# Adjacent weight rows per partition in a decode step with attention and a gated FFN

## The chip, the cores and the metric

The kernel runs on one core of a Trainium2 chip. In the profiles PE is TensorE (PEld its weight loads), DVE VectorE, ACT ScalarE, POOL GpSimd and SP SyncE. The metric is the device time of one launch in microseconds. Most executions of a kernel agree closely; some fall into a slower state, a few us longer at the same work, and are marked as slow (here: over 1.5% above the fastest run of the same kernel). Medians below are of all runs unless fast runs are named. Ratios and their intervals are from fast runs of the same rounds, so they aren't quite the ratio of the medians quoted beside them.

## The reference, cut to what matters

A layer with two parallel branches is run forward and backward: decode attention (4 sequences, one token, 32 query heads, 8 K/V heads, window of 1,024) and a gelu-gated FFN. Outputs are the result and the gradients of x, both caches, wq, wo, w_gate, w_up, w_down.

```python
xn = _layernorm(x)
q = xn @ wq                                   # wq: 512 x 4096
o = softmax(q k^T * 128**-0.5) v              # the last 1024 of 4096 positions
out = x + o @ wo + (gelu(xn @ w_gate) * (xn @ w_up)) @ w_down   # wo: 4096 x 512
# and the vjp of it for grad_out; F = 1792, D = 512, all bf16
```

The cache gradients are zero outside the window: 50 MB of the 81 MB that the kernel writes are zeros.

## The kernel before: the parts that matter

`evac` moves a finished product from PSUM, where TensorE leaves it, to SBUF, the working memory, on ScalarE (ACT) or VectorE (DVE), whichever is less loaded by its own estimate. That estimate counts elements.

```python
def evac(out, in_, n, half=False, eng=None):
    eng = "dve" if half else eng
    ca, cd = (190 + n) / 1.2, (120 + (n / 2 if half else n)) / 0.96
    ...
        last.append(nc.scalar.copy(out=out, in_=in_))
    ...
    return nc.vector.tensor_copy(out=out, in_=in_)

# the small inputs, then the FFN weights; rows 128 apart go to one partition
for eng, dst, src in ((nc.sync, dy_b, grad_out), (nc.scalar, x_b, A_x)):
    eng.dma_start(out=dst[:], in_=bass.AP(tensor=src.tensor, offset=src.offset,
                                          ap=[[D, B], [0, RB], [1, D]]))
nc.sync.dma_start(out=wd_sb[:], in_=B_w_down.rearrange("(c p) n -> p c n", p=P))
nc.sync.dma_start(out=wg_sb[:], in_=B_w_gate.rearrange("(c p) f -> p c f", p=P))
...
# pre(t): do, per head, from the transposed wo
for i in range(2):
    for c in range(ND):
        nc.tensor.matmul(dq_ps[:, 0, 2 * h2 + i, :], lhsT=woT[:, i, c, :], rhs=dyT[:, c, :], ...)
...
# dw_gate, dw_up: one piece of the output rows of chunk c
nc.tensor.matmul(mps[:, 0:n, :]..., lhsT=xnm[:, i, c * P:(c + 1) * P], rhs=s_r[:, 0:n, :]..., ...)
evac(held["osb"][:, 0:n, i, :], mps[:, 0:n, :], n * P)      # runs of 128 elements
```

Zeros are issued on ACT's queue at fixed places of the program, the first at the end of the FFN; loads go out on SP's queue, the other stores on GpSimd's.

## Time and profile before

| | before |
|---|---|
| median of 3 runs | 291.73 us (291.46 to 292.57) |
| profiled execution | span 287.5 us, mean granted clock 0.849 |
| bytes | 112.38 MB at a mean of 391 GB/s |
| end of the FFN (first zeros issued) | 41.16 us |
| last store of dw_up issued | 78.69 us |

The page gives busy shares of each engine, then the span in 40 slices: each digit is a busy share in tenths, and DMA is the mean of the core's 16 DMA engines. Read the DMA row first; the prediction shows it. One line of the costliest groups names the source line, engine, operation, output and input, count, then busy time, mean ns of one, idle time before and its cause.

```profile
L92 ACT CAST osb_g<-dwg_ps 128x384 bf16<-128x384 f32 (+1 forms) x30 | 14.5, 534 | 17.6 <-PE dwg_ps L621 8.1
```

Thirty pieces of dw_gate and dw_up keep ACT busy for 14.5 us; one takes 0.53 us in the mean of both sizes (neighbours overlap a little, so the mean times thirty is more than the busy time).

### The profile page before, as it was taken

The page shows a single profiled execution, that of the slowest core. Times are in us where ns is not written, and L with a number is a line of the kernel's source. Part 1 is how long each engine was busy: PE and PEld are TensorE (multiplying, and loading weights), DVE is VectorE, ACT ScalarE, POOL GpSimd, SP SyncE. Part 2 cuts the span into 40 slices and gives each one's busy share as a digit, 9 for nine tenths or more (in the row PEclk, how much of TensorE's full clock was granted, in tenths as well). Part 3 has the DMA queues.
Part 4 walks back from the last instruction along what each step waited for, and adds up shares of the span by engine and source line. Part 5 has one row for each costly group of instructions (what it writes and reads, how often), then busy time and mean ns, then how long its engine had stood idle before and what let it go on. Part 6 is the DMA issues. An engine that isn't in the chain of part 4 may idle for free.

```text
span 287.5 us, 6821 instructions
## 1 busy us (share of the span) xinstructions
PE 206.9 (72%) x2956; PEld 141.5 (49%) x2956; DVE 144.9 (50%) x310; ACT 113.7 (40%) x217; POOL 66.7 (23%) x84
## 2 busy tenths in 40 slices
PE   1397994983977999545689996546998679597710
PEld 0386882652644765333357654323665355364310
DVE  5484572333564567312626674126476525537770
ACT  1201653443442467312424563134355444336610
POOL 7000130441303152311033323110252132112410
PEclk9996899597897899795958898959799969959975
DMA  5999999999999999999998999999999999999897
GB/s 138 381 389 376 385 399 421 413 403 429 423 426 427 413 372 401 435 415 427 416 419 330 327 363 429 426 427 411 415 413 380 395 390 412 406 415 360 337 393 295
DMA packets 30182, 112.38 MB, mean 391 GB/s; under 512 B 1537, under 2 KB 7689, under 8 KB 26057
## 3 DMA queue, kind: packets, MB, share of 16 engines
q10 hardware_dynamic: 4612, 50.46, 41.9%
q1 hardware_dynamic: 17732, 30.81, 29.4%
q0 software_dynamic: 7808, 30.67, 27.3%
q8 instruction: 23, 0.38, 0.5%
q14 instruction: 7, 0.05, 0.0%
HBM read 30.93 MB, written 81.01 MB: 389 GB/s over the span
## 4 chain that ended last, share of the span: by engine, by line
PE 47%; DMA 28%; DVE 14%; issue 4%; ACT 2%; POOL 1%; SPq 0%; DVEq 0%; ACTq 0%; POOLq 0%
DMA out_dram<-osb_o 14%; PE T_ps L336 9%; PE kv_ps L444 7%; DMA out_dram<-stg_dv 4%; DVE T_sb L94 4%; PE S_ps L341 4%; DMA wd_sb<-in_B_w_down_dram 4%; DMA out_dram<-osb_d 3%; PE od_ps L416 3%; PE woT_ps L288 3%; PE wqT_ps L508 3%; DMA out_dram<-osb_g 2%; PE acc_ps L181 2%; PE wgT_ps L648 2%; PE wdT_ps L536 2%
## 5 line engine op out<-in xcount | busy, mean ns | idle before, releaser
L94 DVE COPY T_sb<-T_ps 128x1024 bf16<-128x1024 bf16 x64 | 44.2, 691 | 34.2 <-PE T_ps L336 33.7
L92 ACT CAST stg_dv<-kv_ps 128x512 bf16<-128x512 f32 x52 | 28.8, 589 | 43.2 <-PE kv_ps L444 42.8
L92 ACT CAST stg_dk<-kv_ps 128x512 bf16<-128x512 f32 x46 | 25.0, 588 | 15.4 <-PE kv_ps L444 13.1
L336 PE MATMUL T_ps<-ident,vb 128*128 128x128 bf16 x256 | 26.1, 251 | 6.6 <-DVE osb_q L94 6.6
L336 PEld LDWEIGHTS <-vb 128*128 128x128 bf16 x256 | 20.0, 114 | 12.7 <-issue 8.9
L92 ACT CAST osb_q<-dwq_ps 128x512 bf16<-128x512 f32 x25 | 13.6, 589 | 30.4 <-DMA out_dram<-osb_o 20.1
L336 PE MATMUL T_ps<-ident,kb 128*128 128x128 bf16 x256 | 24.4, 228 | 0.5 <-ACT stg_dk L92 0.3
L336 PEld LDWEIGHTS <-kb 128*128 128x128 bf16 x256 | 18.1, 101 | 12.4 <-issue 5.0
L444 PE MATMUL kv_ps<-domr,P_q 128*128 128x512 bf16 x64 | 23.9, 435 | 0.0
L444 PE MATMUL kv_ps<-qmr,dS_q 128*128 128x512 bf16 x64 | 20.9, 410 | 1.5 <-ACT stg_dk L92 1.0
L92 ACT CAST osb_g<-dwg_ps 128x384 bf16<-128x384 f32 (+1 forms) x30 | 14.5, 534 | 17.6 <-PE dwg_ps L621 8.1
L94 DVE COPY woT<-woT_ps 128x1024 bf16<-128x1024 bf16 x16 | 11.1, 692 | 17.2 <-PE woT_ps L288 17.2
L478 PE MATMUL dwq_ps<-od_r,xnm 128*128 128x256 bf16 x64 | 12.5, 320 | 6.8 <-DVE osb_q L94 6.6
L352 POOL TENSOR_TENSOR dS_q<-dS_b,qmsk 128x1024 bf16<-128x1024 bf16 x4 | 7.5, 1884 | 34.3 <-DVE dS_b L405 34.3
L92 ACT CAST osb_o<-dwo_ps 128x512 bf16<-128x512 f32 x23 | 12.7, 588 | 7.0 <-PE dwo_ps L463 6.8
L341 PE MATMUL S_ps<-T_sb,dom 128*32 128x256 bf16 x128 | 10.5, 310 | 5.1 <-DVE T_sb L94 5.1
L98 POOL DMA_DIRECT2D out_dram<-osb_q x8 | 5.8, 731 | 34.6 <-ACT osb_q L92 34.6
L94 DVE COPY wqT<-wqT_ps 128x1024 bf16<-128x1024 bf16 x16 | 11.0, 687 | 5.5 <-PE wqT_ps L508 5.3
L508 PEld LDWEIGHTS <-wq_sb 128*128 128x128 bf16 x128 | 11.1, 120 | 5.3 <-issue 4.3
L94 DVE CAST osb_q<-dwq_ps 128x512 bf16<-128x512 f32 x7 | 4.7, 689 | 16.9 <-DMA out_dram<-osb_o 16.9
L98 POOL DMA_DIRECT2D out_dram<-stg_dv x8 | 6.2, 774 | 30.4 <-ACT stg_dv L92 30.4
L94 DVE CAST stg_dk<-kv_ps 128x512 bf16<-128x512 f32 x18 | 12.0, 685 | 2.4 <-PE kv_ps L444 1.2
(187 smaller groups left out, 381.1 us busy)
## 6 DMA issues: line engine op xcount, KB each, us to landing
out_dram<-ztile ACTq DMA_DIRECT2D x8, 3072.0 KB, 16.5
out_dram<-ztile ACTq DMA_DIRECT2D x16, 1536.0 KB, 15.3
kb<-in_A_k_cache_dram SPq DMA_DIRECT2D x8, 1024.0 KB, 17.1
vb<-in_A_v_cache_dram SPq DMA_DIRECT2D x8, 1024.0 KB, 49.5
out_dram<-stg_dv POOLq DMA_DIRECT2D x8, 1024.0 KB, 10.1
out_dram<-stg_dk POOLq DMA_DIRECT2D x8, 1024.0 KB, 8.4
wo_sb<-in_A_wo_dram SPq DMA_DIRECT2D x4, 1024.0 KB, 10.2
wq_sb<-in_A_wq_dram SPq DMA_DIRECT2D x4, 1024.0 KB, 14.2
```

Of the source, the lines that this page charges most:

```text
L92: last.append(nc.scalar.copy(out=out, in_=in_))
L94: return nc.vector.tensor_copy(out=out, in_=in_)
L98: d = eng.dma_start(out=out, in_=in_)
L181: nc.tensor.matmul(ps[:, c, :], lhsT=lf(c), rhs=rhs, start=(k == 0), stop=(k == len(terms) - 1))
L288: nc.tensor.transpose(wT_ps[:, i, c, :], wo_sb[:, 2 * h2 + i, c * P:(c + 1) * P], ident[:])
L336: nc.tensor.transpose(T_ps[:, j, :], blks[(t, g)][:, b, j, :], ident[:])
L341: nc.tensor.matmul(ps[q * RG:(q + 1) * RG, :], lhsT=lf[:, s * RG:(s + 1) * RG], rhs=T_sb[:, q * WQ:(q + 1) * WQ], start=(g == 0 and b == 0 ...
L352: nc.gpsimd.tensor_tensor(out=dst[:], in0=src[:].unsqueeze(1).broadcast_to([P, NQ, WQ]), in1=qmsk[:].unsqueeze(2).broadcast_to([P, NQ, WQ] ...
L416: nc.tensor.matmul(od_ps[b * RB:b * RB + rep, k, g, :], lhsT=pT[:, jj, c0:c0 + rep], rhs=blks[(t, g)][:, b, j, :], start=(j == 0), stop=(j ...
L444: nc.tensor.matmul(mps[:].rearrange("p b d -> p (b d)"), lhsT=src[:, q, jj * P:(jj + 1) * P], rhs=mr[:, g].rearrange("p b d -> p (b d)"), ...
L478: nc.tensor.matmul(mps[:, i].rearrange("p g d -> p (g d)"), lhsT=xnm[:, i2 * 2 + i, c * P:(c + 1) * P], rhs=dq_r[:].rearrange("p g d -> p ...
L508: nc.tensor.transpose(wT_ps[:, i, c, :], wq_sb[:, c, h * Dh:(h + 1) * Dh], ident[:])
```

## The change

The intent is larger transfers. If a partition holds adjacent rows of a weight, they are one contiguous run in memory. So wo gets 8 adjacent rows per partition, w_down 14, w_gate, w_up and wq 4. The price is that the index of a row is now partition times k plus k', and everything that meets this index has to follow it: the columns of w_gate and w_up are taken 14 apart, the outputs dw_gate and dw_up are assembled 14 apart, do is computed as 4 rows, written 8 apart and transposed back, and o is spread over 8 tiles for dwo. Of the two small inputs, x is on ACT's queue already; grad_out joins it there, so that w_down is first on SP's.

```diff
-    for eng, dst, src in ((nc.sync, dy_b, grad_out), (nc.scalar, x_b, A_x)):
-        eng.dma_start(...)
+    for dst, src in ((dy_b, grad_out), (x_b, A_x)):
+        nc.scalar.dma_start(...)
-    nc.sync.dma_start(out=wd_sb[:], in_=B_w_down.rearrange("(c p) n -> p c n", p=P))
+    nc.sync.dma_start(out=wd_sb[:], in_=B_w_down.rearrange("(p c) n -> p c n", p=P))
     ... (w_gate, w_up, wq, wo and the gradients' stores likewise)
+            for c in range(ND):
+                nc.tensor.matmul(do_ps[:, k0:k0 + 2, :], lhsT=dyT[:, c, :], rhs=woT[:, :, c, :], ...)
+            if h2 % 2:
+                evac(do_row[:].rearrange("b (p k) -> b k p", k=HG)[:, 2 * h2 - 2:2 * h2 + 2, :], do_ps[:], 512,
+                     eng=("act", "dve")[h2 // 2])
+        for h in range(HG):
+            nc.tensor.transpose(doT_ps[:, h, :], do_row[:, h * Dh:(h + 1) * Dh], ident[0:B, 0:B])
     ... (o: four masked copies into X, eight products with qmsk)
-                nc.tensor.matmul(h_ps[:, fc, :], lhsT=wsb[:, c, fc * P:(fc + 1) * P], rhs=xnT[:, c, :],
+                nc.tensor.matmul(h_ps[:, fc, :], lhsT=wsb[:, c, fc:F:NF], rhs=xnT[:, c, :],
-        evac(held["osb"][:, 0:n, i, :], mps[:, 0:n, :], n * P)
+        evac(held["osb"][:].rearrange("p (d k) -> p k d", k=NF)[:, i:NF:4, :], mps[:, 0:n, :], n * P)
```

More of the change, by code (lines that the diff above doesn't have):

```diff
@@ L65 @@
     CW = HG * Dh
-    assert Sq == 1 and Dh == P and D == 512 and F % P == 0 and RG == 32 and JQ * NQ == J and WQ == JQ * P
+    assert NQ == B == rep and Sq == 1 and Dh == P and D == 512 and F % P == 0 and RG == 32 and JQ * NQ == J and WQ == JQ * P
     scale = float(Dh) ** -0.5
@@ L111 @@
     dy_b = const.tile([P, D], BF16, name="dy_b")
-    for eng, dst, src in ((nc.sync, dy_b, grad_out), (nc.scalar, x_b, A_x)):
-        eng.dma_start(out=dst[:], in_=bass.AP(tensor=src.tensor, offset=src.offset,
-                                                  ap=[[D, B], [0, RB], [1, D]]))
+    for dst, src in ((dy_b, grad_out), (x_b, A_x)):
+        nc.scalar.dma_start(out=dst[:], in_=bass.AP(tensor=src.tensor, offset=src.offset,
+                                                    ap=[[D, B], [0, RB], [1, D]]))
     wd_sb = ffn_w.tile([P, NF, D], BF16, name="wd_sb")
-    nc.sync.dma_start(out=wd_sb[:], in_=B_w_down.rearrange("(c p) n -> p c n", p=P))
+    nc.sync.dma_start(out=wd_sb[:], in_=B_w_down.rearrange("(p c) n -> p c n", p=P))
     wg_sb = ffn_w.tile([P, ND, F], BF16, name="wg_sb")
-    nc.sync.dma_start(out=wg_sb[:], in_=B_w_gate.rearrange("(c p) f -> p c f", p=P))
+    nc.sync.dma_start(out=wg_sb[:], in_=B_w_gate.rearrange("(p c) f -> p c f", p=P))
     wu_sb = ffn_w.tile([P, ND, F], BF16, name="wu_sb")
-    nc.sync.dma_start(out=wu_sb[:], in_=B_w_up.rearrange("(c p) f -> p c f", p=P))
+    nc.sync.dma_start(out=wu_sb[:], in_=B_w_up.rearrange("(p c) f -> p c f", p=P))
     ident = const.tile([P, P], BF16, name="ident")
@@ L205 @@
     dyT = const.tile([P, ND, B], BF16, name="dyT")
-    for src, dstT in ((dy_b, dyT), (xn_b, xnT)):
+    for src, dstT, adj in ((dy_b, dyT, False), (xn_b, xnT, True)):
         tps = ps_x.tile([P, ND, P], BF16, name="tps", tag="x")
         for c in range(ND):
-            nc.tensor.transpose(tps[:, c, :], src[:, c * P:(c + 1) * P], ident[:])
+            nc.tensor.transpose(tps[:, c, :], src[:, c:D:ND] if adj else src[:, c * P:(c + 1) * P], ident[:])
         nc.vector.tensor_copy(out=dstT[:], in_=tps[:].rearrange("p c (b r) -> p c b r", b=B)[:, :, :, 0])
     xnm = const.tile([P, rep, D], BF16, name="xnm")
-    dym = const.tile([P, rep, D], BF16, name="dym")
+    dym = ffn.tile([P, rep, D], BF16, name="dym")
     for src, dst in ((dy_b, dym), (xn_b, xnm)):
@@ L218 @@
                                     op0=ALU.mult)
-    wo_v = A_wo.rearrange("(t h p) n -> t p h n", p=P, h=HG)
-    wq_v = A_wq.rearrange("(c p) (t j) -> t p c j", p=P, j=CW)
+    wo_v = A_wo.rearrange("(t p k) n -> t p k n", p=P, k=HG)
+    wq_v = A_wq.rearrange("(p c) (t j) -> t p c j", p=P, j=CW)
     wo_t, wq_t, k_t, v_t = {}, {}, {}, {}
@@ L282, in pre @@
         wo_sb, wq_sb = wo_t[t], wq_t[t]
-        dq_ps = ps_x.tile([P, 2, HG, B], FP32, name="doq_ps", tag="x")
+        do_row = attw.tile([B, CW], BF16, name="do_row", tag="do_row", bufs=1)
         for h2 in range(HG // 2):
+            if h2 % 2 == 0:
+                do_ps = (ps_x, ps_w)[h2 // 2].tile([B, rep, P], FP32, name="do_ps", tag="xw"[h2 // 2])
             wT_ps = ps_w.tile([P, 2, ND, P], BF16, name="woT_ps", tag="w")
@@ L290, in pre @@
             evac(woT[:], wT_ps[:], 1024, half=True)
-            for i in range(2):
-                for c in range(ND):
-                    nc.tensor.matmul(dq_ps[:, 0, 2 * h2 + i, :], lhsT=woT[:, i, c, :], rhs=dyT[:, c, :],
-                                     start=(c == 0), stop=(c == ND - 1))
+            k0 = 2 * (h2 % 2)
+            for c in range(ND):
+                nc.tensor.matmul(do_ps[:, k0:k0 + 2, :], lhsT=dyT[:, c, :], rhs=woT[:, :, c, :],
+                                 start=(c == 0), stop=(c == ND - 1))
+            if h2 % 2:
+                evac(do_row[:].rearrange("b (p k) -> b k p", k=HG)[:, 2 * h2 - 2:2 * h2 + 2, :], do_ps[:], 512,
+                     eng=("act", "dve")[h2 // 2])
             tick(2)
+        dq_ps = ps_x.tile([P, HG, B], FP32, name="dq_ps", tag="x")
         for h in range(HG):
             for c in range(ND):
-                nc.tensor.matmul(dq_ps[:, 1, h, :], lhsT=wq_sb[:, c, h * Dh:(h + 1) * Dh], rhs=xnT[:, c, :],
+                nc.tensor.matmul(dq_ps[:, h, :], lhsT=wq_sb[:, c, h * Dh:(h + 1) * Dh], rhs=xnT[:, c, :],
                                  start=(c == 0), stop=(c == ND - 1))
+        doT_ps = ps_w.tile([P, HG, B], BF16, name="doT_ps", tag="w")
+        for h in range(HG):
+            nc.tensor.transpose(doT_ps[:, h, :], do_row[:, h * Dh:(h + 1) * Dh], ident[0:B, 0:B])
         T4 = []
@@ L302, in pre @@
             xT4 = attw.tile([P, NQ, B, HG], BF16, name=nm + "T4", tag=nm + "T4")
-            src = dq_ps[:, k].rearrange("p h b -> p b h").unsqueeze(1).broadcast_to([P, NQ, B, HG])
+            src = (doT_ps, dq_ps)[k][:].rearrange("p h b -> p b h").unsqueeze(1).broadcast_to([P, NQ, B, HG])
             if sc is None:
@@ L418, in odq @@
                                      tile_position=(0, b * RB))
-        rows = attw.tile([P, GP, Dh], BF16, name="od_r", tag=f"od_r{k}")
         if k == 0:
-            nc.vector.tensor_copy(out=rows[:], in_=od_ps[:, k])
-        else:
-            nc.scalar.activation(out=rows[:], in_=od_ps[:, k], func=ACT.Copy, scale=scale)
+            X = attw.tile([P, HG, GP, rep, P // HG], BF16, name="o_x", tag="o_x", bufs=1)
+            for i in range(rep):
+                src = od_ps[:, 0].rearrange("p g (e k) -> p k g e", k=HG)
+                if i % 2:
+                    nc.scalar.activation(out=X[:, :, :, i, :], in_=src, func=ACT.Copy, scale=msk_i[:, i:i + 1])
+                else:
+                    nc.vector.tensor_scalar(out=X[:, :, :, i, :], in0=src, scalar1=msk_i[:, i:i + 1], scalar2=None,
+                                            op0=ALU.mult)
+            X = X[:].rearrange("p k g i e -> p k (g i e)")
+            oT_ps = ps_w.tile([P, HG, B], FP32, name="oT_ps", tag="w")
+            for h in range(HG):
+                nc.tensor.matmul(oT_ps[:, h, :], lhsT=X[:, h, :], rhs=qmsk[:], start=True, stop=True)
+            oT = attw.tile([P, HG, B], BF16, name="oT", tag="oT")
+            nc.vector.tensor_copy(out=oT[:], in_=oT_ps[:])
+            st[t]["o"] = X, oT
+            return
+        rows = attw.tile([P, GP, Dh], BF16, name="od_r", tag="od_r")
+        nc.scalar.activation(out=rows[:], in_=od_ps[:, 1], func=ACT.Copy, scale=scale)
         T_ps = ps_w.tile([P, GP, P], BF16, name="odT_ps", tag="w")
@@ L426, in odq @@
             nc.tensor.transpose(T_ps[:, g, :], rows[:, g, :], ident[:])
-        rT = attw.tile([P, GP, rep, B], BF16, name="od_T", tag=f"od_T{k}")
+        rT = attw.tile([P, GP, rep, B], BF16, name="od_T", tag="od_T")
         nc.vector.tensor_copy(out=rT[:],
                               in_=T_ps[:].rearrange("p g (b r) -> p g r b", b=B)[:, :, 0:rep, :])
-        st[t][("o", "dq")[k]] = rows, rT
+        st[t]["dq"] = rows, rT
     def dvdk(t, k):
@@ L455, in dw @@
     def dw(t):
-        o_r, dq_r = st[t]["o"][0], st[t]["dq"][0]
+        X, dq_r = st[t]["o"][0], st[t]["dq"][0]
         def piece_o(g, i, held):
@@ L462, in piece_o @@
             mps = ps_w.tile([P, D], FP32, name="dwo_ps", tag="w")
-            nc.tensor.matmul(mps[:], lhsT=o_r[:, g, :], rhs=dym[:, i, :], start=True, stop=True)
+            nc.tensor.matmul(mps[:], lhsT=X[:, g * rep + i, :], rhs=dy_b[:], start=True, stop=True)
             evac(held["osb"][:, i, :], mps[:], 512)
             if i == rep - 1:
-                r0 = (t * HG + g * rep) * Dh
-                store(nc.gpsimd, out=out_5[r0:r0 + rep * Dh, :].rearrange("(h p) n -> p h n", p=P),
-                                    in_=held["osb"][:], kind="rest",
+                store(nc.gpsimd, out=out_5[t * CW:(t + 1) * CW, :].rearrange("(p k) n -> p k n", k=HG)[
+                    :, g * rep:(g + 1) * rep, :], in_=held["osb"][:], kind="rest",
                           apart=["zeros", "rest"])
@@ L478, in piece_q @@
                 nc.tensor.matmul(mps[:, i].rearrange("p g d -> p (g d)"),
-                                 lhsT=xnm[:, i2 * 2 + i, c * P:(c + 1) * P],
+                                 lhsT=xnm[:, i2 * 2 + i, c:D:ND],
                                  rhs=dq_r[:].rearrange("p g d -> p (g d)"), start=True, stop=True)
@@ L482, in piece_q @@
             if k == 3:
-                store(nc.gpsimd, out=out_4[c2 * 2 * P:(c2 + 1) * 2 * P, t * CW:(t + 1) * CW].rearrange("(c p) j -> p c j", p=P),
+                store(nc.gpsimd, out=out_4.rearrange("(p c) j -> p c j", c=ND)[:, c2 * 2:(c2 + 1) * 2, t * CW:(t + 1) * CW],
                     in_=held["osb"][:].rearrange("p c g i d -> p c (g i d)"), kind="rest",
@@ L500, in fin @@
         wo_sb, wq_sb = wo_t.pop(t), wq_t.pop(t)
-        acc_sum(0, [(lambda c, h=h: wo_sb[:, h, c * P:(c + 1) * P], oT[:, h // rep, h % rep, :]) for h in range(HG)])
+        acc_sum(0, [(lambda c, h=h: wo_sb[:, h, c * P:(c + 1) * P], oT[:, h, :]) for h in range(HG)])
         wT = []
@@ L611, in piece_d @@
         if i == n - 1:
-            store(nc.gpsimd, out=out_8[4 * f4 * P:(4 * f4 + n) * P, :].rearrange("(h p) n -> p h n", p=P),
+            store(nc.gpsimd, out=out_8.rearrange("(p k) n -> p k n", k=NF)[:, 4 * f4:4 * f4 + n, :],
                                 in_=held["osb"][:, 0:n, :], kind="rest",
@@ L617, in piece_g @@
         if i == 0:
-            held["osb"] = outp.tile([P, NF4, 4, P], BF16, name="osb_g", tag="o")
+            held["osb"] = outp.tile([P, F], BF16, name="osb_g", tag="o")
         n = (NF - i + 3) // 4
         mps = ps_w.tile([P, NF4, P], FP32, name="dwg_ps", tag="w")
-        nc.tensor.matmul(mps[:, 0:n, :].rearrange("p f d -> p (f d)"), lhsT=xnm[:, i, c * P:(c + 1) * P],
+        nc.tensor.matmul(mps[:, 0:n, :].rearrange("p f d -> p (f d)"), lhsT=xnm[:, i, c:D:ND],
                          rhs=s_r[:, 0:n, :].rearrange("p f d -> p (f d)"), start=True, stop=True)
-        evac(held["osb"][:, 0:n, i, :], mps[:, 0:n, :], n * P)
+        evac(held["osb"][:].rearrange("p (d k) -> p k d", k=NF)[:, i:NF:4, :], mps[:, 0:n, :], n * P)
         if i == 3:
-            store(nc.gpsimd, out=og[c * P:(c + 1) * P, :],
-                                in_=held["osb"][:].rearrange("p f i d -> p (f i d)")[:, 0:F], kind="rest",
+            store(nc.gpsimd, out=og.rearrange("(p c) f -> p c f", c=ND)[:, c, :],
+                                in_=held["osb"][:], kind="rest",
                       apart=["zeros", "rest"])
@@ L647 @@
                 for c in range(ND):
-                    nc.tensor.transpose(wT_ps[:, i, c, :], wsb[:, c, fc * P:(fc + 1) * P], ident[:])
+                    nc.tensor.transpose(wT_ps[:, i, c, :], wsb[:, c, fc:F:NF], ident[:])
             wgT = tsb.tile([P, 2, ND, P], BF16, name="wgT", tag="wT")
@@ L698, with adj @@
                 nc.tensor.transpose(f_ps[:, c, :], acc_r[:, o, c].rearrange("p b r -> p (b r)"), ident_f[:])
-            fin_ps.append(f_ps[:].rearrange("p c d -> p (c d)"))
-        acc_o, acc_d = fin_ps
+            fin_ps.append(f_ps[:])
+        acc_o, acc_d = fin_ps[0].rearrange("p c d -> p (c d)"), fin_ps[1].rearrange("p c d -> p d c")
+        def adj(x):
+            return x[:].rearrange("p (d c) -> p d c", c=ND)
         out_b = kvp.tile([P, D], BF16, name="out_b", tag="vb")
@@ L705 @@
         s1 = const.tile([P, 1], FP32, name="s1")
-        nc.vector.reduce_sum(out=s1[:], in_=acc_d, axis=AX.X)
+        nc.vector.reduce_sum(out=s1[:], in_=acc_d, axis=AX.XY)
         pr = kvp.tile([P, D], FP32, name="pr", tag="vb")
         s2 = const.tile([P, 1], FP32, name="s2")
-        nc.vector.tensor_tensor_reduce(out=pr[:], in0=acc_d, in1=xn_f[:], scale=1.0, scalar=0.0,
+        nc.vector.tensor_tensor_reduce(out=adj(pr), in0=acc_d, in1=adj(xn_f), scale=1.0, scalar=0.0,
                                        op0=ALU.mult, op1=ALU.add, accum_out=s2[:])
@@ L714 @@
         nc.vector.tensor_scalar(out=nm2[:], in0=s2[:], scalar1=-1.0 / D, scalar2=None, op0=ALU.mult)
-        nc.vector.scalar_tensor_tensor(out=pr[:], in0=xn_f[:], scalar=nm2[:, 0:1], in1=acc_d,
+        nc.vector.scalar_tensor_tensor(out=adj(pr), in0=adj(xn_f), scalar=nm2[:, 0:1], in1=acc_d,
                                        op0=ALU.mult, op1=ALU.add)
```

## The prediction

> **What bounds the kernel now.** I read the page top down: engines (PE, the busiest, is at 72%), slices, queues, chain. The lines that decide are the slices and the queues (packets, MB, share of 16 engines' span).
>
> ```profile
> DMA  5999999999999999999998999999999999999897
> GB/s 138 381 389 376 385 399 421 413 403 429 423 426 427 413 372 401 435 415 427 416 419 330 327 363 429 426 427 411 415 413 380 395 390 412 406 415 360 337 393 295
> ...
> q10 hardware_dynamic: 4612, 50.46, 41.9%
> q1 hardware_dynamic: 17732, 30.81, 29.4%
> q0 software_dynamic: 7808, 30.67, 27.3%
> ```
>
> The reader is to see that the DMA row is 9 almost throughout and that the queues' shares sum to about 99%. So the transfers bound the kernel, and the rate tells how well they run: 376 to 389 GB/s in slices 2 to 5, where only loads run, 420 to 430 where zeros dominate. q10 is ACT's queue (zeros), q1 SP's (loads), q0 GpSimd's (other stores). Next, the chain in order of time, for compute waiting on transfers:
>
> ```profile
> 113.48 17.92 DMA out_dram<-osb_o
> ...
> 170.73 19.11 DMA out_dram<-osb_o
> ```
>
> In these two pieces alone (start, length, what) compute stood 37 us behind output tiles whose stores were under way. Compute has slack; lost DMA time has none. Third, the start in the timeline, because the change reorders it:
>
> ```profile
> 0.81 0.72 SPq L113 DMA_DIRECT2D dy_b<-in_grad_out_dram  x1
> 0.81 1.43 ACTq L113 DMA_DIRECT2D x_b<-in_A_x_dram  x1
> ...
> 4.99 0.61 PE L209 MATMUL tps<-ident,dy_b 128*128 128x128 bf16 x4 [0.54 <-DMA dy_b<-in_grad_out_dram]
> ...
> 6.99 0.69 DVE L190 BATCH_NORM_STATS2 stats<-x_b 128x6 f32<-128x512 bf16 x1 [1.62 <-DMA x_b<-in_A_x_dram]
> ...
> 12.09 2.21 PE L536 MATMUL wdT_ps<-ident,wd_sb 128*128 128x128 bf16 x19 [6.50 <-DMA wd_sb<-in_B_w_down_dram]
> ```
>
> grad_out is usable at 4.99 us, x at 6.99, w_down at 12.09: w_down opens the FFN. Its end, same view:
>
> ```profile
> 32.84 0.92 POOL L98 DMA_DIRECT2D out_dram<-osb_d  x1 [26.48 <-ACT osb_d L92]
> ...
> 41.16 0.73 ACTq L98 DMA_DIRECT2D out_dram<-ztile  x1
> ```
>
> Until the first dw_down store at 32.84 the DMA engines have only the opening loads to do: grad_out, x and eleven more (three FFN weights, wo, wq, six of K and V). The next load, wo of the second stage, waits for the memory of the FFN weights (issued at 40.93), and the first zeros are issued with the FFN's last step (41.16). Last, the queues in the stretch 50 to 55 us:
>
> ```profile
> q10 hardware_dynamic: 117, 1.44, 67.6%
> q0 software_dynamic: 102, 0.53, 25.5%
> q1 hardware_dynamic: 118, 0.12, 6.9%
> ```
>
> 117 packets of ACT's queue beside 118 of SP's, though theirs are 12 KB and 1 KB: the queues take turns by packet, not by byte.
>
> **What the Trainium skill says.** "DMA: Bandwidth & Descriptors", Queues, rings and completion order: each engine goes round robin over the queues "at *packet* granularity". The trace agrees (117 to 118). Same page, Why a DMA increments its semaphore by 16: the number of engines divides the slowest dimension of both patterns. grad_out and x are read with a slowest dimension of 4, so 4 engines. In the DMA view of 0 to 7 us the first data slices (2.3 to 4.2 us) move 59 to 123 GB/s; four engines at 1 KB per 50 ns (worked out below) would be 82: it fits. Same page, Why small descriptors are slow: a fixed cost per packet; the trace gives its size below. "SBUF — State Buffer", Door 1: The DMA port swizzle: 16-byte lines, with a penalty for reads that use one element of each. Strided weight reads of 28 bytes are new here, so no row of this trace speaks to it.
>
> **The change part by part.** *Packet cost.* Packet time is share x 287.5 x 16. q1: 1,352 us over 17,732 packets, 76 ns at 1,738 B. q10: 1,927 us over 4,612, 418 ns at 10,941 B. Two equations: about 12 ns each plus 0.0371 ns per byte; so 1 KB 50 ns, 2 KB 88, 8 KB 316, 14 KB 544.
>
> *Loads, removed.* One contiguous run is one packet (zeros: 12,288 B, 4,096 packets of q10's 4,612). wo: 4,096 packets of 1 KB become 512 of 8 KB; w_down 1,792 become 128 of 14 KB; w_gate and w_up 1,024 become 256 of 14 KB. 6,016 packets fewer x 12 ns / 16 engines = 4.5 us. wq stays at 2 KB runs: a column slice of rows that are adjacent is not contiguous.
>
> *Stores.* dwo and dw_down rows of 1 KB become 4 KB runs. But q0 already averages 30.67 MB / 7,808 = 3.9 KB per packet although no store row exceeds 3.5 KB: it is packed already. I count 0.
>
> *do.* Per stage 32 narrow products (0.34 us per 8) give way to 16 wide ones, two small evictions (0.59 us ACT, 0.69 DVE) and 8 small transposes: by estimate +1 us PE, +1.3 us on the two others, four times, most of it in slack. *o spread.* One copy of 0.42 us becomes four of about 0.4 on two engines, and two transposes become 8 small products: +1 us, four times, partly hidden. dwo keeps 8 products. Together I allow 1 us on the end.
>
> *Start, moved.* This is where I chose. w_down, w_gate and w_up now give SP's queue 8 packets each of 544 ns per engine. grad_out and x both move to ACT's queue: 32 packets each of 1 KB on the same 4 engines, and each has to take turns with one packet of SP's. Say SP's first data flow at 2.3 us as now (first slice with data in that view) and ACT's at 4, since x lands no earlier today. By 4 about 3 weight packets are gone; 21 turns of 544 + 50 ns take 12.5 us; 8 turns against wo (316 + 50) 2.9 us; 3 against wq (138 ns) 0.4. grad_out lands at about 19.8 us. x's 32 packets against wq at 138 ns: 4.4 us more, 24.2. With the 0.6 us that a landing takes to be seen, x is usable near 24.8 instead of 6.99. w_down itself is there at about 7.5, and useless: hg and the derivative of gelu need x, dym needs grad_out, and VectorE works in order, its statistics of x ahead of the w_down evictions.
>
> *What that does.* Today VectorE goes from the first w_down eviction (13.17) to hg (20.94); after, it begins at 24.8 with statistics, dyT and dym (2.2 us), then the seven evictions (4.8) and xn (2.3): hg at about 34, 13 us late. If the w_down part runs ahead of x, hg still needs statistics, normalisation, transposes and 56 products (4.7 us): 29.5, 8.5 us late. So the FFN ends 8.5 to 13 us late, and with it the next load, about 49.5 to 54 (plus 1.5 us to first data, 51 to 55.5). Work for the DMA engines until then: after the change the opening loads are 384 packets at 544 ns, 128 at 316 (wo), 3,584 at 88 (wq, K, V) and 256 at 50: 578 us over 16 engines, 36.1 us. The dw_down stores are 1.84 MB, 4.7 us at the mean 391 GB/s. From 2.3 us on that lasts to about 43. Hole: 8 to 12.5 us, in which no transfer has anything to do.
>
> Sum: -4.5 (packets) - 0.7 (fuller start, an estimate from slice 1's 138 GB/s) + 8 to 12.5 (hole) + 1 (do and o) = +3.8 to +8.3 us; on the measured 291.7 that is 295.5 to 300.
>
> **The rivals.** (A) x is not late: if ACT's small packets reached the engines before w_down's, everything shrinks to -4.5 - 0.7 + 1, about 287.5, and with w_down earlier perhaps 285. For it: SP and ACT issue at the same time, and somebody put w_down first on purpose. Against: taking turns by packet is what the 117 to 118 shows, and a turn cannot be skipped. (B) Compute catches up and hides the hole. For: 37 us of compute slack. Against: the hole is in the DMA, which has none; zeros are tied to ACT's instruction order and cannot move forward. Time: as in the sum. (C) Strided weights: 112 products and 112 transposes read weight columns 28 B apart, the strided evictions of dw_gate and dw_up write so too. Transposes are 59 ns apart now, the up products 25 (0.47 us per 8 and 1.15 us per 46 in the chain). If a load costs 50 ns the products lose 2.8 us and the transposes little; in the late FFN this adds to the hole: up to 303. (D) SP loads shorten but stores wait: another -2 if 1 KB rows inside q0's packets were slower. Time: 294 to 298.
>
> **Range and chances.** I give late x 75 to 80%, though the argument is strong, since the start of ACT's queue is inferred from one load. In that case 295 to 301, about half of it above the 2% line of 297.6; else 284 to 289, about half of it below 285.9. The middle of both is 296, the range 285 to 302. Faster 0.12, within 2% 0.43, slower 0.45.
>
> **What would show it.** Late x: the statistics wait on x_b until 20 to 25 us and the w_down products wait no longer on w_down; the DMA row has slices under 5 between 36 and 55 us; first dw_down store after 41 us. Packets: q1 falls by about 6,000 to 11,700, slices 2 to 5 near 410 GB/s. Stores: q0 stays near 7,800. Wrong if x_b lands before 10 us; then rival A's time holds. If x is late and the DMA row stays at 9, my hole is wrong; if up products or wgT take much longer each, C.

## The result, and the profile after

The changed kernel takes 358.62 us (median of 4 runs, 357.52 to 364.08) against 291.6 (291.04 to 292.57) in the same rounds: a ratio of 1.23 (95% interval 1.2233 to 1.2367), 67 us slower. The prediction said 296, with a range to 302.

Here are the slices and queues after, to lay beside those of before:

```profile
DMA  8999415992286876359999956999997389999896
GB/s 303 395 329 388 172 62 184 384 401 103 104 352 279 352 302 273 119 175 388 421 418 424 416 212 198 357 429 423 395 430 316 117 332 416 387 409 409 341 403 246
...
q10 hardware_dynamic: 4744, 50.60, 33.8%
q1 hardware_dynamic: 11584, 30.68, 24.2%
q0 software_dynamic: 7808, 30.67, 21.8%
```

The row of nines is gone. The transfers still move 112.38 MB, but the DMA engines are partly idle in four places: slices 5 to 7 (36 to 63 us), slices 10 to 18 (80 to 161 us), and shorter ones at slices 24 and 25 and at 31 and 32. SP's queue lost 6,148 packets, GpSimd's none, both as predicted. Which work ran in the holes is told by the start, in the timeline:

```profile
21.29 0.60 PE L210 MATMUL tps<-ident,dy_b 128*128 128x128 bf16 x4 [16.85 <-DMA dy_b<-in_grad_out_dram]
...
26.31 0.69 DVE L191 BATCH_NORM_STATS2 stats<-x_b 128x6 f32<-128x512 bf16 x1 [20.94 <-DMA x_b<-in_A_x_dram]
```

grad_out is usable at 21.29 us instead of 4.99, x at 26.31 instead of 6.99. And by the chain of work that ended last, in order of time (start, length, what):

```profile
2.03 24.26 DMA x_b<-in_A_x_dram
...
84.35 6.61 ACT osb_g L94 x4
...
92.06 7.23 ACT osb_g L94 x4
...
140.37 2.43 ACT do_row L94
```

Before, the chain's long pieces were stores of output tiles. Now they are evictions on ACT. The group that cost 14.5 us is the second of the page:

```profile
L94 ACT CAST osb_g<-dwg_ps 128x512 bf16<-128x512 f32 (+1 forms) x30 | 59.0, 2375 | 4.7 <-PE dwg_ps L645 4.7
```

The same count of nearly the same sizes takes 59.0 us: 2.4 us each in the mean in place of 0.53. The evictions of do, which are new, cost as much (count, then shortest, median and longest in ns, first and last start in us):

```profile
L94 ACT CAST do_row<-do_ps x4: 2416/2426/2737, 63.7 to 270.4; 4x512 bf16<-4x512 f32 x4
L96 DVE CAST do_row<-do_ps x4: 2406/2407/2422, 75.8 to 276.1; 4x512 bf16<-4x512 f32 x4
```

Where the time came in can be read off the issue times of the same steps in both timelines:

| step | before | after | shift |
|---|---|---|---|
| first zeros (end of the FFN) | 41.16 | 58.75 | +17.6 |
| last store of dw_up | 78.69 | 127.72 | +49.0 |
| last store of stage 1's dwq (first of four stages) | 133.78 | 189.12 | +55.3 |
| the same, second stage | 191.78 | 255.63 | +63.9 |
| the same, third stage | 241.20 | 310.08 | +68.9 |
| the same, fourth stage | 276.36 | 345.32 | +69.0 |

So 17.6 us are lost at the start, 31.4 in the stretch of dw_gate and dw_up, and 20 more over the first three stages, in each of which do is prepared for the next.

### The profile page after: what moved, and what is told of

Same layout as the page of the kernel before. It is cut to its first block, busy times and chain, and to the rows that moved or that the text cites. A ratio compares the mean times of both kernels' runs of the same rounds, so it can differ in the third digit from the quotient of the medians.

```text
span 357.7 us, 6810 instructions
## 1 busy us (share of the span) xinstructions
PE 231.7 (65%) x2935; PEld 156.7 (44%) x2948; DVE 159.5 (45%) x318; ACT 169.6 (47%) x229; POOL 64.6 (18%) x84
## 2 busy tenths in 40 slices
DMA packets 24165, 112.38 MB, mean 314 GB/s; under 512 B 1536, under 2 KB 1800, under 8 KB 19144
## 3 DMA queue, kind: packets, MB, share of 16 engines
q1 hardware_dynamic: 11584, 30.68, 24.2%
q0 software_dynamic: 7808, 30.67, 21.8%
## 4 chain that ended last, share of the span: by engine, by line
PE 42%; DMA 21%; ACT 16%; DVE 13%; issue 5%; ACTq 0%; DVEq 0%; POOLq 0%
ACT osb_g L94 11%; PE T_ps L346 8%; DMA out_dram<-osb_o 8%; DMA x_b<-in_A_x_dram 7%; PE kv_ps L469 6%; DMA out_dram<-stg_dv 4%; PE S_ps L351 3%; DVE T_sb L96 3%; DMA out_dram<-ztile 3%; PE do_ps L296 3%; PE wgT_ps L672 2%; PE wqT_ps L532 2%; PE woT_ps L291 2%; DVE do_row L96 2%; ACT do_row L94 2%
## 5 line engine op out<-in xcount | busy, mean ns | idle before, releaser
L96 DVE COPY T_sb<-T_ps 128x1024 bf16<-128x1024 bf16 x64 | 44.4, 694 | 57.5 <-PE T_ps L346 57.2
L94 ACT CAST osb_g<-dwg_ps 128x512 bf16<-128x512 f32 (+1 forms) x30 | 59.0, 2375 | 4.7 <-PE dwg_ps L645 4.7
L346 PE MATMUL T_ps<-ident,vb 128*128 128x128 bf16 x256 | 27.7, 260 | 20.0 <-DVE osb_q L96 10.2
L346 PEld LDWEIGHTS <-vb 128*128 128x128 bf16 x256 | 21.3, 118 | 27.9 <-issue 24.2
L346 PE MATMUL T_ps<-ident,kb 128*128 128x128 bf16 x256 | 26.1, 241 | 8.5 <-ACT osb_g L94 7.9
L346 PEld LDWEIGHTS <-kb 128*128 128x128 bf16 x256 | 19.5, 107 | 20.8 <-issue 14.7
L469 PE MATMUL kv_ps<-domr,P_q 128*128 128x512 bf16 x59 | 23.0, 445 | 0.9 <-issue 0.9
L94 ACT CAST osb_o<-dwo_ps 128x512 bf16<-128x512 f32 x23 | 12.7, 589 | 7.4 <-PE dwo_ps L488 7.1
L100 POOL DMA_DIRECT2D out_dram<-osb_g x8 | 4.4, 552 | 54.1 <-ACT osb_g L94 44.2
L532 PE MATMUL wqT_ps<-ident,wq_sb 128*128 128x128 bf16 x128 | 13.6, 271 | 0.1
L502 PE MATMUL dwq_ps<-od_r,xnm 128*128 128x256 bf16 x64 | 13.4, 338 | 0.2
L296 PE MATMUL do_ps<-woT,dyT 128*4 128x256 bf16 x64 | 12.0, 321 | 1.6 <-DVE woT L96 1.6
## 6 DMA issues: line engine op xcount, KB each, us to landing
kb<-in_A_k_cache_dram SPq DMA_DIRECT2D x8, 1024.0 KB, 14.5
```

The lines of the kernel that those rows point to most:

```text
L100: d = eng.dma_start(out=out, in_=in_)
L296: nc.tensor.matmul(do_ps[:, k0:k0 + 2, :], lhsT=dyT[:, c, :], rhs=woT[:, :, c, :], start=(c == 0), stop=(c == ND - 1))
L346: nc.tensor.transpose(T_ps[:, j, :], blks[(t, g)][:, b, j, :], ident[:])
L469: nc.tensor.matmul(mps[:].rearrange("p b d -> p (b d)"), lhsT=src[:, q, jj * P:(jj + 1) * P], rhs=mr[:, g].rearrange("p b d -> p (b d)"), ...
L502: nc.tensor.matmul(mps[:, i].rearrange("p g d -> p (g d)"), lhsT=xnm[:, i2 * 2 + i, c:D:ND], rhs=dq_r[:].rearrange("p g d -> p (g d)"), st ...
L532: nc.tensor.transpose(wT_ps[:, i, c, :], wq_sb[:, c, h * Dh:(h + 1) * Dh], ident[:])
```

## The experiments

**Three suspects, each undone alone, then together.** Theory T: three separate costs add up, x late, the evictions of dw_gate and dw_up written 28 B apart, the evictions of do written 16 B apart. The rivals (lettered anew, these aren't the prediction's): late x drives all (A), the hole at the start is filled up again (B), weights read with a step cost it (C), the do chain lies in slack (D).

Run x_first moves only the issue of the small inputs, to SP's queue ahead of the weights:

```diff
-        nc.scalar.dma_start(out=dst[:], in_=bass.AP(tensor=src.tensor, ...
+        nc.sync.dma_start(out=dst[:], in_=bass.AP(tensor=src.tensor, ...
```

> The changed kernel with grad_out and x both issued on SP's queue ahead of w_down (undoes only that part). Theory T (three separate costs add up: x late by 19 us, dw_gate/dw_up evictions written 28 B apart, do evictions written 16 B apart): x usable before 8 us, first zeros issued about 13 us earlier than the 58.75 us of the changed kernel, whole time 358.6 - 13 = 345 us (342 to 349). Rival A (late x alone drives the loss, the rest follows from it): under 310 us. Rival B (the hole at the start is filled up again later): 356 to 360.

It takes 346.44 us (345.03 to 348.56), ratio 1.1949 to before. The wait of VectorE for x is 1.0 us instead of 20.9, the first zeros go out at 42.41 us. That is 12 us of the 67, as theory T has it; rivals A and B are out.

Run osb_flat writes the dw_gate and dw_up evictions contiguously. Columns come out in the wrong order; number, size and stores are the same.

```diff
-        evac(held["osb"][:].rearrange("p (d k) -> p k d", k=NF)[:, i:NF:4, :], mps[:, 0:n, :], n * P)
+        evac(held["osb"][:].rearrange("p (k d) -> p k d", k=NF)[:, i:NF:4, :], mps[:, 0:n, :], n * P)
```

> The changed kernel with the evictions of dw_gate and dw_up written contiguously (columns in the wrong order on purpose; same number of elements, same stores). Theory T: one eviction falls from 2.2 us to 0.55 on ACT, the stretch from the first zeros to the last dw_up store shrinks from 69 to about 38 us, whole time about 327 us (323 to 333). Rival A (late x drives it): 355 or more. Rival C (weights read 28 B apart on PE are the cost, not the writes): evictions short but time above 350 us.

It takes 331.71 us; its fast runs are 329.70, 330.74 and 332.69, ratio 1.1422. In the profile of it (a slow run; the evictions of do, which it leaves as they are, take 2.417 us on ACT in it and 2.426 in the fast profile of x_first) the same thirty evictions read (shortest, median, longest in ns):

```profile
L94 ACT CAST osb_g<-dwg_ps x30: 458/585/803, 60.1 to 98.1; 128x512 bf16<-128x512 f32 x15, 128x384 bf16<-128x384 f32 x15
```

The stretch from first zeros to last dw_up store shrinks from 69 us to 39.6 (59.27 to 98.84). Only the write pattern was changed, so it is the writes: 28 us. Rival C is out.

Run do_flat does the same to the two evictions of do (do in the wrong order):

```diff
-                evac(do_row[:].rearrange("b (p k) -> b k p", k=HG)[:, 2 * h2 - 2:2 * h2 + 2, :], do_ps[:], 512,
+                evac(do_row[:].rearrange("b (k p) -> b k p", k=HG)[:, 2 * h2 - 2:2 * h2 + 2, :], do_ps[:], 512,
```

> The changed kernel with the two evictions of do per stage written contiguously (do in the wrong order on purpose). Theory T: 2.42 us become 0.59 (ACT) and 0.69 (DVE); each of the three later stages loses 6 us less, whole time about 340 us (336 to 346). Rival D (the do chain lies in compute slack): 355 us or more.

It takes 336.79 us (335.10 to 337.87, all fast), ratio 1.1615. The evictions take 0.574 us on ACT and 0.679 on DVE. Eight short instructions are worth 22 us, more than the 8 x 1.8 = 14.4 us by which they got shorter. The timeline of the changed kernel shows where more can come from:

```profile
142.84 0.56 PE L305 MATMUL dq_ps<-xnT,wq_sb 128*128 128x4 bf16 x17 [1.96 <-ACT do_row L94]
```

The products of dq wait 1.96 us for do_row on ACT, because both use the one bank of their pool, and products of the V gradient and the next transposes queue behind them on PE. That this makes up the whole difference was not tested. Rival D is out.

Run three has all three edits:

> All three edits together (wrong results on purpose). Theory T: 358.6 - 13 - 31 - 19 = 296 us (289 to 302), slow remainder from weights read 28 B apart (hg and hu 3.4 us instead of 1.5) and longer chains. If the parts overlap, it stays above 305; if the packets' 4.5 us are really won, it may reach 288.

It takes 293.66 us; one run of four was fast, 289.27. Before took 288.53 to 291.44 in its fast runs of the same rounds. The three edits together win back all of the 67 us within the noise (by the medians of all runs, 293.66 against 290.84, some 3 us are left): the cause of the result is settled. Singly they sum to 12 + 28 + 22 = 62. These differences cross rounds; by the ratios to before they are about 10, 25 and 20, so the single shares are good to 2 or 3 us.

**How a write's cost depends on its step.** The bench run appends copies of 128x512 from PSUM to the changed kernel, two of each kind on each engine. It was run once, so its total says nothing, but its single copies can be compared with each other. Its edit is, in short:

```diff
+        for s in (1, 2, 4, 7, 8, 14):
+            one(f"w{s}x", lambda t_, s=s: t_[:, 0:512 * s:s], 512 * s)       # bf16, step s
+        one("f7x", lambda t_: t_[:, 0:512 * 7:7], 512 * 7, FP32)               # fp32, step 7
+        one("rd4x", ..., inp=src[:].rearrange("p (k d) -> p d k", k=4))        # read with a step
+        one("run4x", ...)   # written in runs of 4 elements, 16 B apart, read with a step
+        one("in8x", ...)    # written 8 B apart inside each 28 B, read with a step
```

> The changed kernel with copies of 128x512 from PSUM appended at its end, two of each kind on ACT and on DVE: bf16 written at steps of 1, 2, 4, 7, 8, 14 elements, fp32 at step 7, read at a step of 4 and written contiguously, written in runs of 4, and written 8 B apart in the order of addresses. Theory T1 (every single 2-byte write apart from the last costs, whatever the step): step 2 already near 2.4 us, runs of 4 near 0.6 to 1. Theory T2 (cost comes with leaving a 16-byte line): step 2 and 4 cheap (0.6 to 1.2), step 8 and 14 2.4 us. Theory T3 (partial words: writes under 4 bytes cost): fp32 at step 7 stays 0.6 us. Reading at a step is cheap in all (0.6).

ACT's part of its timeline, where each row is two copies (the length is of both together):

```profile
346.98 1.20 ACT L761 CAST baw1x<-bsrc 128x512 bf16<-128x512 f32 x2 [0.86 <-DVE bsrc L753]
352.69 1.48 ACT L761 CAST baw2x<-bsrc 128x512 bf16<-128x512 f32 x2 [4.50 <-DVE bvw1x L763]
355.78 2.61 ACT L761 CAST baw4x<-bsrc 128x512 bf16<-128x512 f32 x2 [1.61 <-DVE bvw2x L763]
361.12 4.31 ACT L761 CAST baw7x<-bsrc 128x512 bf16<-128x512 f32 x2 [2.73 <-DVE bvw4x L763]
369.86 4.87 ACT L761 CAST baw8x<-bsrc 128x512 bf16<-128x512 f32 x2 [4.43 <-DVE bvw7x L763]
380.01 4.72 ACT L761 CAST baw14x<-bsrc 128x512 bf16<-128x512 f32 x2 [5.28 <-DVE bvw8x L763]
389.57 2.16 ACT L761 COPY baf7x<-bsrc 128x512 f32<-128x512 f32 x2 [4.84 <-DVE bvw14x L763]
394.02 1.20 ACT L761 CAST bard4x<-bsrc 128x512 bf16<-128x512 f32 x2 [2.28 <-DVE bvf7x L763]
396.76 1.20 ACT L761 CAST barun4x<-bsrc 128x512 bf16<-128x512 f32 x2 [1.54 <-DVE bvrd4x L763]
399.49 2.33 ACT L761 CAST bain8x<-bsrc 128x512 bf16<-128x512 f32 x2 [1.53 <-DVE bvrun4x L763]
```

Count how often the writes of one copy go to another 16-byte line, per partition, a line that they come back to being counted again; call it a visit: 128 at step 2, 256 at step 4, 448 at step 7, 512 from step 8 on, 224 in the last row. The medians of single copies are 0.726, 1.289, 2.138, 2.420 and 1.148 us. From one to the next, (1.289 - 0.726) / 128 and (2.420 - 1.289) / 256 both give 4.4 ns per visit, and the last row, 0.726 + 96 x 4.4 ns, comes out at 1.148. So single 2-byte writes cost 4.4 ns per visit (step 14 is slightly under it at 2.345). DVE has the same values from step 2 on. Step 2 is 0.726, not 2.4, so T1 is out. It is T2 in kind: what counts is how often the writes change line. But step 4 is already twice the contiguous 0.585, which T2 had as cheap, and T3 is half right too: 4-byte elements 28 B apart (fp32 at step 7) cost 1.065 us where 2-byte ones 28 B apart (step 14) cost 2.345. Runs of 4 elements (8 bytes) and reads from PSUM with a step cost nothing extra. Four partitions cost do_row as much as 128 would.

**The same result with the loops exchanged.** Run swap keeps the values of the changed kernel and writes in the order of addresses:

```diff
-                evac(do_row[:].rearrange("b (p k) -> b k p", k=HG)[:, 2 * h2 - 2:2 * h2 + 2, :], do_ps[:], 512,
+                evac(do_row[:].rearrange("b (p k) -> b p k", k=HG)[:, :, 2 * h2 - 2:2 * h2 + 2],
+                     do_ps[:].rearrange("b k p -> b p k"), 512,
-        evac(held["osb"][:].rearrange("p (d k) -> p k d", k=NF)[:, i:NF:4, :], mps[:, 0:n, :], n * P)
+        evac(held["osb"][:].rearrange("p (d k) -> p d k", k=NF)[:, :, i:NF:4],
+             mps[:, 0:n, :].rearrange("p f d -> p d f"), n * P)
```

> The changed kernel, same result, with the loops of both strided evictions exchanged so that the writes run in the order of addresses: do in runs of 4 elements (8 bytes) at 16 B, dw_gate and dw_up elements 8 B apart inside each 28 B. If the cost is per jump to another line (T2): do evictions 0.7 to 1, dw_gate 0.7 to 1.2, time about 358.6 - 19 - 25 = 315. If it is per separate piece written (T1): do evictions near 0.7 to 1 (quarter of the pieces), dw_gate unchanged at 2.2, time about 340. If reading PSUM at a step of 512 B costs as much: no change, 356 or more.

The fast runs are 313.02 and 315.83 us (all four: 313.02 to 320.42), the result is correct. do's evictions take 0.574 us on ACT, dw_gate's 1.225 in the median. By size, dw_gate's and dw_up's are (profile of a slow run; busy time, mean ns of one, idle time before):

```profile
L94 ACT CAST osb_g<-dwg_ps 128x512 bf16<-128x512 f32 x15 | 16.7, 1217 | 3.3 <-PE dwg_ps L646 3.0 <-DMA out_dram<-osb_g 0.3
L94 ACT CAST osb_g<-dwg_ps 128x384 bf16<-128x384 f32 x15 | 16.6, 1244 | 0.2 <-PE dwg_ps L646 0.2
```

The lines touched are the same as before the exchange; the visits are not. For an eviction of dw_gate they fall from 512 (128x512) or 384 (128x384) to 224 for both sizes, and the two sizes now take the same time, though one has a third more elements. So the reading by visits holds inside the kernel. A changed loop order, with no other edit, gives back some 44 of the 67 us (two fast runs only; ratio to before 1.083, interval 1.0474 to 1.1185).

**Why x was late.** Run before_act makes only this move in the kernel before: both small inputs on ACT's queue, w_down first on SP's, with its old 1 KB rows.

```diff
-    for eng, dst, src in ((nc.sync, dy_b, grad_out), (nc.scalar, x_b, A_x)):
+    for eng, dst, src in ((nc.scalar, dy_b, grad_out), (nc.scalar, x_b, A_x)):
```

> The kernel before with only the issue of grad_out moved to ACT's queue ahead of x, so w_down is first on SP, with its old 1 KB rows. Theory (queues take turns by packet, so what makes x late is the 14 KB of SP's packets): 64 turns of about 100 ns, x usable at 9 to 12 us, w_down at about 11, time 290 to 293. Rival (ACT's queue is simply slow or served last): x usable after 18 us and time 300 or more.

It takes 289.71 us (289.26 to 291.65), ratio 0.9995 with an interval of 0.9815 to 1.0175, so the late issue costs nothing that can be seen here. The start in its timeline:

```profile
8.83 0.60 PE L209 MATMUL tps<-ident,dy_b 128*128 128x128 bf16 x4 [4.38 <-DMA dy_b<-in_grad_out_dram]
12.66 0.69 DVE L190 BATCH_NORM_STATS2 stats<-x_b 128x6 f32<-128x512 bf16 x1 [7.29 <-DMA x_b<-in_A_x_dram]
```

The same queues in the same order, and x is usable at 12.66 us instead of 26.31 (a little over the 9 to 12 that I expected). What differs is the size of the packets that it takes turns with, 1 KB or 14 KB.

**What is left if only the good parts stay?** Run f_plain has x first on SP, w_down rows and FFN columns as before, do in runs of 4, and keeps the adjacent rows of wo, w_gate, w_up and wq, with a correct result. Its edits beyond x_first and swap's do:

```diff
-B_w_down.rearrange("(p c) n -> p c n", p=P)     lhsT=wsb[:, c, fc:F:NF]
+B_w_down.rearrange("(c p) n -> p c n", p=P)     lhsT=wsb[:, c, fc * P:(fc + 1) * P]
     (and the transposes, the evictions and the store of dw_down likewise)
```

> A version meant to keep only what pays, with the right result: grad_out and x first on SP; w_down rows and FFN columns as before (so evictions contiguous and weights read contiguously), w_gate, w_up, wq and wo rows adjacent, do evictions in runs of 4. Theory T: packets fewer by 4,352, 3.3 us of DMA; do chain still a little longer: 286 to 292 us, x usable before 8 us, no DMA slice under 8 between 10 and 250 us. If wide do and the o spread cost on the path more than I think: 293 to 300.

295.63 us in the median of six, but five runs were slow; the one fast run is 290.12, and before's fast runs beside it span 288.54 to 292.67. No gain can be seen. Two runs split it: load_only keeps the adjacent rows of w_gate, w_up and wq alone, do_only those of wo with the new do and o (both with x first).

> The kernel before with only w_gate, w_up and wq rows adjacent (4 per partition; 768 packets fewer, 0.6 us of DMA) and grad_out and x both first on SP; wo, do, o and w_down as before. If the 295.6 us of the cleaned version came from the new do and o work: 289 to 291.5 us here, same as before within 0.5%. If it came from the adjacent rows of D (weights read 8 B apart, the tail) or from x on SP: 294 to 297.

> The kernel before with only wo rows adjacent (3,584 packets fewer, 2.7 us of DMA), the new do (its two evictions per stage in runs of 4) and the o spread, and grad_out and x first on SP. If the new do and o lie on the path where no zeros are left to send (a hole near 215 to 230 us): 293 to 298 us with the hole. If they lie in slack: 287 to 289.

load_only: 291.28 us, ratio 0.9978 (0.9902 to 1.0054). do_only: 293.35 us, ratio 1.0043 (0.9967 to 1.0118). Neither differs from before beyond its interval. The profile of do_only shows the hole that was asked for: in 215 to 225 us its DMA share is 0.57, against 1.02 in load_only and 0.95 in before. In f_plain it is 0.47. The profiles of do_only and f_plain are of slow runs; how large the hole is in a fast one isn't known. The columns here are the stretch, its length, the busy time of PE, PEld, DVE, ACT and POOL, the clock, DMA share and GB/s:

```profile
215.00:225.00 10.00, 9.44 (x153) 6.82 (x153) 7.43 (x17) 5.56 (x12) 5.28 (x4) 1.00 0.47 179
```

PE is busy 9.44 of 10 us while no zeros are queued. So f_zero moves four zero blocks ahead of this stage in f_plain, and before_zero is the control on the kernel before:

```diff
-            zeros(2 if t >= NT - 2 else 0)
+            zeros({NT - 2: 6, NT - 1: 2}.get(t, 0))
```

> The cleaned version of before with four more zero blocks (3 MB, about 7 us of transfers) issued ahead of the last stage's preparation, where it has a hole of about 5 us, taken from those left for the end. If the hole is what eats its gain: DMA share near 1 from 215 to 225 us and 286 to 290 us in fast runs, 1% under the kernel before. If the chain of compute sets the end by itself: no change, 290 to 293.

> The control: the same four zero blocks moved in the kernel before, which has no such hole. 290 to 292 us, same as before within 0.5%. If moving zeros forward pays by itself (shorter tail), it gains as much as the cleaned version: 286 to 289.

f_zero: 291.67 us, ratio 1.0025 (0.9966 to 1.0085). before_zero: 291.91 us, ratio 1.0034 (0.9968 to 1.01). In f_zero the hole is filled, and the end is emptied:

```profile
215.00:225.00 10.00, 8.36 (x112) 5.28 (x113) 6.16 (x10) 5.56 (x11) 1.54 (x2) 1.00 1.01 421
...
275.00:291.00 16.00, 5.28 (x29) 3.52 (x27) 8.80 (x17) 4.14 (x8) 3.39 (x5) 0.71 0.52 198
```

The transfers are then done early and the last evictions and stores end no sooner. I read this as the compute chain setting the end; before_zero, with a share of 0.56 in the same last stretch, fits, but no run shortens that chain to test it. I found no version that beats the kernel before.

## Why the prediction was wrong

Step by step, in its order:

- **What bounds the kernel.** The shares were read rightly: the DMA engines of the kernel before are busy throughout. That transfers alone set its end isn't shown; no run made them much shorter. I carried "compute has slack" over to a kernel whose evictions I hadn't priced.
- **Packets.** The counts were right: SP's 11,584 for "about 11,700", GpSimd's 7,808 for 7,808. So was the cost of one. The traces hold the packets with size and time: in the kernel before, SP's 1 KB packets take 50.7 ns in the mean and its 3.5 KB ones 145.8, which makes 12.7 ns each plus 0.0371 ns per byte, and the 14 KB ones of load_only take 543 for "544". The rate at the start rises with it: 425 GB/s where 14 KB packets run alone (run three, 6 to 14 us), 367 where mostly w_down's 1 KB packets do in the kernel before (8 to 11.5 us). The saving is what failed. In run three, with 5,884 packets fewer, the FFN weights and wo take 25.1 us of the 16 engines instead of 28.0, so 2.9 of the "4.5"; wo's 8 KB packets take 364 ns for "316". And the packets of wq, K and V, which stay at 2 KB, take 57.5 us instead of 55.9, and x, now on this queue, 0.4. SP's packets take 83.7 us in all, for 84.6 before. The sum had let every packet keep its time whatever else was sent; why those of wq, K and V take longer is open (the fast profile of load_only has it too, 57.3 us). None of it shows on the end in load_only, do_only or f_plain. Slices 2 to 5 aren't "near 410 GB/s" but 395, 329, 388 and 172.
- **Start.** The mechanism and most sizes were right: grad_out "at about 19.8" plus 0.6 against 21.29, x "near 24.8" against 26.31. ACT's first packet came at 5.9 us, not at 4, and a landing was seen 0.85 us after its last packet, not 0.6. The FFN ended 17.6 us late instead of 8.5 to 13. The prediction's rival C is in it: hg's and hu's 56 products, with weights read 28 B apart, took 3.4 us each on the chain instead of 1.5 and 1.7. But x_first has the same products and its first zeros come only 1.3 us later than before's, so no run isolates this share. Undoing the move made the FFN end 16.3 us earlier and the kernel 12, inside the hole of "8 to 12.5".
- **do.** "Two small evictions (0.59 us ACT, 0.69 DVE)": they took 2.42 each. This term failed. It was priced from rows with contiguous writes; "most of it in slack" failed with it, for do_flat won 22 us against the "1 us on the end" that I allowed.
- **dw_gate and dw_up.** This is the step that did most harm. The sum has no term for it. Rival C says that the "strided evictions of dw_gate and dw_up write so too" and then prices only the weight reads. The passage of the Trainium skill that the prediction names ("SBUF — State Buffer", Door 1: The DMA port swizzle) speaks of accesses to 16-byte lines; the prediction took it for reads alone, and in these runs writes pay, 4.4 ns per visit. Thirty-two evictions of about 0.53 us became 2.4 us, and that took 28 us on the end.

The measured parts, 12 + 28 + 22 us from undoing each, stand against a sum of +3.8 to +8.3. The direction, the late x and the first hole were foreseen; the range failed on two write patterns.

## What to carry to other kernels

A new layout has to be priced where its index is written, not only where it is loaded: before believing in bigger packets, go through every eviction and ask how often its writes go to another 16-byte line. If an interleaved output can't be avoided, order the loops so that neighbouring elements are written together; reads from PSUM with a step were free here. A small load that gates the start doesn't belong on a queue that takes turns with 14 KB packets: put it ahead on the same queue.

## What the Trainium skill lacked or had wrong

- "SBUF — State Buffer", Door 1: The DMA port swizzle, has bf16 strides up to 8 elements as free. For ACT's and DVE's writes they aren't: 512 elements took 0.585 us contiguously on ACT, 0.726 at step 2, 1.289 at step 4 and 2.420 at step 8. Its 16-byte line is the right unit: 4.4 ns for each time that single 2-byte writes change line. 4-byte elements 28 B apart took 1.065 us where 2-byte ones took 2.345; the section doesn't price either.
- "TensorE: Matmul & The Clock Gate", Weight-path perf modes, lists strided weights as a pattern of the fast load without a price. 56 products with weights 28 B apart took 3.36 us in the chain of the changed kernel; with contiguous ones 1.54 us in the timeline of the kernel before.
- "DMA: Bandwidth & Descriptors", Queues, rings and completion order, gives the turn by packet but not what it does to a small load: the same 128 KB were usable at 12.66 us beside 1 KB packets and at 26.31 us beside 14 KB ones.
